# One input tile that holds the last odd pair's strip too, so that a PSUM bank is evacuated in one operation

## The chip, the cores and the metric

The kernel runs on one NeuronCore of a Trainium2 chip. Its engines have instruction queues of their own, worked off in order: TensorE (PE) for matmuls into the PSUM banks, VectorE (DVE), ScalarE (ACT) and GpSimd (POOL) for everything elementwise, SyncE (SP) for issuing DMAs. They wait for one another on semaphores, which a tile framework sets from the tiles that instructions read and write. The metric is the device time of one execution in microseconds, as the median of several runs.

## What is computed

A decaying linear attention, then a first feed-forward layer ("expert") with SiLU, then a second one with a softmax-gated, normalised hidden layer. Inputs: q, k, v, alpha of shape (4, 8, 768, 48), weights (384, 2048), (2048, 384), (384, 1024), (1024, 384) and a gain of 1024. Cut to what matters:

```python
# attention, all float32, for each batch b and head h:
state = 0
for t in range(S):                                   # S = 768, D = 48
    state = alpha[t][:, None] * state + outer(k[t], v[t])
    y[t] = q[t] @ state
x = y as (3072 tokens, 384)
h = x @ w_in;  x = (h * sigmoid(h)) @ w_out          # first expert, 384 -> 2048 -> 384
h = x @ w2_in                                        # second expert, 384 -> 1024 -> 384
e = exp(h - max(h));  solu = h * e / (sum(e) + 1e-9)
ln = (solu - mean(solu)) / sqrt(var(solu) + 1e-6) * g_ln
out = ln @ w2_out
```

## The kernel before

**Attention in chunks.** The 3072 tokens are 24 chunks of 128. For each chunk the class Chunk transposes k (L540), forms scores (L559), masks them, carries the state (L593, L595) and writes the attention's output transposed, heads along the partitions, into two PSUM banks: `y[0]` (bank sA) holds the head pairs 0 and 2, `y[1]` (bank sB) the odd pairs 1 and 3, each as 112 rows by two strips of 128 columns. `evac` (L640, ScalarE) copies a bank to SBUF rounded to the matmul's type, `rest` (L644, VectorE) subtracts that copy from the bank, which leaves the low part: every value is kept as a high and a low half, and each product takes three matmuls.

**Where the output goes.** The first expert reads an input of 384 rows as three blocks of 128 partitions. The 112 rows of a pair leave 16 rows free behind each 48, and the fourth pair is cut up to fill them. `y_all` holds these inputs for two units at a time; a unit is 256 or 384 tokens, eleven in all (UNITS). Bank sA's two strips go straight to blocks 0 and 2 of `y_all`, in one operation of each engine. Of bank sB the first strip goes to block 1, and the second, the last odd pair, to a small tile of its own, `yt`, from which `holes` (L651) copies it by six DMAs into the free rows. So bank sB takes two operations on ScalarE and two on VectorE per chunk (`places`).

**First expert.** For each unit and each of 16 slices of 128 hidden features, `h_groups` makes nine matmuls (L736 to L738), two SiLU activations (L742, L743) and one subtraction for the low half (L746); `x_groups`, two slices later, makes nine matmuls into three accumulators (L771 to L773). After a unit's last slice the accumulators are copied to `x_all` (L779 on VectorE, L781 on ScalarE) and stored to HBM as `x2d[u]` (L783, SyncE). The last unit alone is copied to a tile `x2s` in the pool of the second expert's weights, all three parts by VectorE.

**The order.** The first four units' work is written out by hand in the table ORDER; from there on a chunk's steps are spread evenly between the matmul groups of the unit before. With the last unit the attention's pools are closed and the second expert's weights are loaded (`weight_steps`): eight pieces of 768 KB in a raw form, each loaded by SyncE (L899), converted by ScalarE (L87, L115), VectorE (L93, merge L120), split into high (L932, ScalarE) and low (L937, VectorE). These steps are spread between the matmul groups of the last unit. A raw piece needs a buffer until its merge; two of three lie in the stage pool and every third one uses the space of `x_all` ("spare"), so that piece i + 3 is loaded when piece i is merged.

**Second expert.** 24 tiles of 128 tokens, in an order given by the words HEAD, BODY and TAIL: load and split the input (x; L974, L975), hidden layer (h; 18 matmuls L986 to L988), maximum (m; L146), exponential (e; L149, ScalarE), centring (c; L156 to L162, VectorE), squares (q; L165), factor (f), transposes of the centred tile (t; L1011), high and low copies of them (a, b), output (o; 24 matmuls L1032 to L1034) and store (s). HEAD begins with e0 h1 c0 x2 q0 m1 f0 t0 a0 e1; h0 and m0 are put six matmul groups ahead of the first expert's end. The pool of `y_all`, `x_all` and the SiLU tiles (mw) is closed behind the last group, and the working tiles of the second expert (pool pb: e, s, c, ct and so on) are laid over its space.

Of the kernel before, what the change touches and what calls it, by code (L numbers as in the profile page):

```python
# [4 lines left out]
F32 = mybir.dt.float32  # L5
F32R = mybir.dt.float32r
# [3 lines left out]
U32 = mybir.dt.uint32  # L10
# [9 lines left out]
CH = 128  # L20
HP = 112
# [5 lines left out]
KC, KF, KB = DM // 128, DFF // 128, DF2 // 128  # L27
PW = 768
N1, N2 = 8, 4
W0, W1 = 256, 384  # L30
# [34 lines left out]
NU = len(UNITS)  # L65
# [18 lines left out]
def rebias(nc, f, raw):  # L84


    nc.scalar.mul(f, raw[:, :, 1].bitcast(F32), 2.0**-112)  # L87


def unsign(nc, f, raw=None):  # L90

    if raw is None:
        nc.vector.scalar_tensor_tensor(out=f, in0=f, scalar=-(2.0**32), in1=f, op0=ALU.mult, op1=ALU.max)  # L93
    else:
        spare = raw[:, :, 1].bitcast(F32)
        nc.scalar.activation(out=spare, in_=f, func=AF.Relu, scale=-(2.0**32))
        nc.gpsimd.tensor_tensor(out=f, in0=f, in1=spare, op=ALU.add)
# [15 lines left out]
def low_bits(nc, raw):  # L113

    nc.scalar.mul(raw[:, :, 0], raw[:, :, 0], 2.0**-29 * 0.936)  # L115


def merge(nc, f, raw):
    b = f.bitcast(U32)
    nc.vector.scalar_tensor_tensor(  # L120
        out=b, in0=b, scalar=3, in1=raw[:, :, 0], op0=ALU.logical_shift_left, op1=ALU.bitwise_or
    )
# [7 lines left out]
def words(w):  # L130
    return w.bitcast(U32).rearrange("p (n t) -> p n t", t=2)


class Norm:


    def __init__(self, nc, p, h2, mhalf, tag):
        self.nc, self.p, self.h2, self.mhalf, self.tag = nc, p, h2, mhalf, tag
# [196 lines left out]
def main(tc, const, ident, mask, flags, ones, mhalf, good, x2d,  # L335
# [4 lines left out]
    def push(name):  # L340
        cm = tc.tile_pool(name=name, bufs=1, side="right")
        right.append(cm)
        return cm.__enter__()

    def pop():
        right.pop().__exit__(None, None, None)

    stage, att = push("stage1"), push("att")
# [3 lines left out]
    mw = mw_cm.__enter__()  # L352
# [8 lines left out]
    spare = psh.tile([128, 512], F32, tag="h", name="spare")  # L361
# [8 lines left out]
    v_t, y_t, yt_t, st_t = {}, {}, {}, {}  # L370
# [24 lines left out]
    for t in ms:  # L395
        nc.gpsimd.memset(t, 0.0)

    y_all = mw.tile([128, 2 * KC * 2 * W1], F32R, name="y_all")
    x_all = mw.tile([128, 2 * KC * W0], F32, name="x_all")

    def y_of(u):
        n = UNITS[u][2]
        o = u * KC * 2 * n if u < WIDE else (u - WIDE) % 2 * KC * 2 * n
        return y_all[:, o : o + KC * 2 * n].rearrange("p (k h n) -> p k h n", k=KC, h=2)

    x2s = {}

    def xs_of(u):
        n = UNITS[u][2]
        if u == NU - 1:  # L410
            if "last" not in x2s:
                x2s["last"] = phb.w2.tile([128, KC, n], F32, name="x2s")
            return x2s["last"]
        o = u % 2 * KC * n if u < WIDE else 0
        return x_all[:, o : o + KC * n].rearrange("p (k n) -> p k n", k=KC)

# [103 lines left out]
    class Chunk:  # L520
# [101 lines left out]
        def places(self, k):  # L622

            u, at = self.u, slice(self.at, self.at + CH)
            if u not in y_t:
                y_t[u] = y_of(u)
                yt_t[u] = att.tile([HP, 2, W1], F32R, tag="yt", bufs=1, name="yt")
            y = self.y[k][:HP]
            if k == 0:
                dst = y_t[u][:HP, 0:3:2]  # L630
                return [(y[:, : 2 * CH].rearrange("p (k n) -> p k n", k=2), dst[:, :, 0, at], dst[:, :, 1, at])]
            dst, yt = y_t[u][:HP, 1], yt_t[u]
            return [
                (y[:, CH : 2 * CH], yt[:, 0, at], yt[:, 1, at]),
                (y[:, :CH], dst[:, 0, at], dst[:, 1, at]),
            ]

        def evac(self, k):
            for y, hi, _ in self.places(k):
# [164 lines left out]
    at = {}  # L804
# [8 lines left out]
    phb = None  # L813
    k0 = 0
    for word in ORDER.split():
        letter, i, other = word[0], int(word[1:].rstrip("*")), word[-1] == "*"
# [6 lines left out]
    phb = None  # L823
    for k, (gi, fn) in enumerate(groups):
        if k < k0:
            continue
        fn()
        for s in per.get(k, []):
            s()
        if gi == NG and psh_cm:  # L830
            psh_cm.__exit__(None, None, None)
            psh_cm = None
            phb.open_late(psx)
            nc.scalar.activation(out=act0, in_=act0, func=AF.Exp)
        if phb is None and gi == start[NU - 1] + LAG + 1:
            phb = PhaseB(tc, const, flags, ones, mhalf, good, ident, x2d, w2_in, w2_out, g_ln, out, stage, x_all)
            phb.check(psa)
            psa_cm.__exit__(None, None, None)
            pop()
            pop()  # L840
            phb.stage = push("stage2")
            phb.open_early()
            per.setdefault(len(groups) - 1 - EARLY, []).append(lambda: (phb.h2(0), phb.top(0)))
            ws = phb.weight_steps()
            for i, w in enumerate(ws):
                per.setdefault(k + 1 + (len(groups) - 20 - k) * i // len(ws), []).append(w)
# [7 lines left out]


class PhaseB:
    def __init__(self, tc, const, flags, ones, mhalf, good, ident, x2d, w2_in, w2_out, g_ln, out, stage, spare):
        self.__dict__.update(locals())
        self.nc = tc.nc
        self.cms = []  # L860
# [24 lines left out]
    def weight_steps(self):  # L885
        nc, w2, stage = self.nc, self.w2, self.stage
        self.w2i = w2.tile([128, 2, KC, DF2], F32R, name="w2i")
        self.w2o = w2.tile([128, 2, KB, DM], F32R, name="w2o")
        gl = w2.tile([128, KB], F32, name="gl")
        nc.sync.dma_start(out=gl, in_=self.g_ln)  # L890
        raws = {}

        def load(i):
            if i < 2 * N2:
                if i % 3 == 2:
                    raws[i] = words(self.spare[:, : 2 * PW])
                else:
                    raws[i] = stage.tile([128, PW, 2], U32, tag="raw", bufs=2, name="raw")
                nc.sync.dma_start(out=raws[i], in_=words((self.w2_out if i % 2 else self.w2_in)[i // 2]))  # L899

        fs, parts = {}, {}

        def start(i):
            fs[i] = stage.tile([128, PW], F32, tag="f", bufs=3, name="f")
            rebias(nc, fs[i], raws[i])

        def signed(i):
            low_bits(nc, raws[i])
            unsign(nc, fs[i])

        def joined(i):
            merge(nc, fs[i], raws.pop(i))
            load(i + 3)

        def gained(i):
            if i % 2:
                for j in range(2):
                    k = i // 2 * 2 + j
                    h = fs[i][:, j * DM : j * DM + DM]
                    nc.vector.tensor_scalar_mul(h, h, gl[:, k : k + 1])  # L920

        def split(i):
            f = fs.pop(i)
            if i % 2 == 0:
                k = i // 2 * 256
                hi, lo = (self.w2i[:, q, :, k : k + 256] for q in range(2))
                f = f.rearrange("p (k f) -> p k f", k=KC)
            else:
                k = i // 2 * 2
                hi, lo = (self.w2o[:, q, k : k + 2, :] for q in range(2))  # L930
                f = f.rearrange("p (k f) -> p k f", k=2)
            nc.scalar.copy(hi, f)  # L932
            parts[i] = f, hi, lo

        def lows(i):
            f, hi, lo = parts.pop(i)
            nc.vector.tensor_tensor(out=lo, in0=f, in1=hi.bitcast(F32), op=ALU.subtract)  # L937

        for i in range(3):
            load(i)  # L940
        r = [lambda: None] * 3
        for k in range(2 * N2 + 2):
            for d, fn in ((2, split), (1, signed), (1, joined), (2, lows), (1, gained), (0, start)):
                if 0 <= k - d < 2 * N2:
                    r.append(lambda fn=fn, i=k - d: fn(i))
        return r + [self.first_tiles]
# [184 lines left out]
```

## Time and profile before

| what | us |
|---|---|
| median of three runs (753.98 to 754.39) | 754.22 |
| the profiled execution | 754.29 |
| its span, first to last instruction | 752.5 |
| TensorE busy | 726.6 |
| VectorE busy | 401.7 |
| ScalarE busy | 342.2 |
| GpSimd busy | 147.1 |

The span is what the trace shows; the profiled execution's own time is 1.8 us longer. Busy time counts an engine's instructions while they run, waits not. In a row of a timeline the first two numbers are the start and the duration in microseconds, and what stands in square brackets is the idle time of the engine just before, with whoever ended it. A row "xN" stands for N instructions of a kind that follow each other.

### The profile page before, as it was taken

To read this page: it belongs to the slowest core of one execution; us is meant where nothing else is said; L and a number is where in the kernel's file an instruction comes from. 1 tells how busy PE (TensorE), PEld (TensorE's weight loads), DVE (VectorE), ACT (ScalarE), POOL (GpSimd) and SP (SyncE) were. 2 spreads that over 40 slices of the span, in tenths; PEclk is the share of its full clock that TensorE was granted. 3 is DMA by queue.
4 is the path that set the end of the run, shared out by engine and by line. 5 is a ranking of instruction groups with operands and counts; after the bars stand their busy time and mean duration, and the time that the engine had idled before them with its cause. 6 is when DMAs were issued, how large, how long until landed. Compare 5 with 4: busy or idle time off the path is not lost.

```text
span 752.5 us, 13157 instructions
## 1 busy us (share of the span) xinstructions
PE 726.6 (97%) x5282; PEld 682.2 (91%) x5282; DVE 401.7 (53%) x728; ACT 342.2 (45%) x731; POOL 147.1 (20%) x199
## 2 busy tenths in 40 slices
PE   4779999999999999999999999999999999999996
PEld 3679999999999999999999999999899999999996
DVE  6998963264435335433544422485755555555552
ACT  5768743344344333334333433584544444444442
POOL 4432431222112111111111100001211111111110
PEclk9899999999999999999999999999999999999999
DMA  8645522032122121211402100541211111111001
GB/s 345 206 166 205 183 87 75 13 111 75 54 70 85 54 69 53 86 25 46 138 3 68 43 1 17 203 165 43 74 43 44 42 43 43 43 44 42 32 22 37
DMA packets 27094, 60.11 MB, mean 80 GB/s; under 512 B 3089, under 2 KB 19025, under 8 KB 27025
## 3 DMA queue, kind: packets, MB, share of 16 engines
q1 hardware_dynamic: 26000, 56.28, 21.9%
q10 hardware_dynamic: 1024, 2.92, 1.2%
q8 instruction: 43, 0.70, 0.4%
q14 instruction: 27, 0.21, 0.1%
HBM read 47.39 MB, written 9.44 MB: 76 GB/s over the span
## 4 chain that ended last, share of the span: by engine, by line
PE 92%; DVE 3%; DMA 1%; ACT 1%; issue 1%; POOL 1%; SPq 0%; ACTq 0%; DVEq 0%; POOLq 0%
PE h L736 9%; PE x L771 9%; PE x L773 9%; PE h L738 9%; PE h L737 9%; PE x L772 9%; PE o L1032 5%; PE o L1033 4%; PE h L987 4%; PE h L986 4%; PE o L1034 4%; PE h L988 4%; PE sA L559 3%; PE tp L1011 3%; PE sA L610 1%; PE sA L617 1%
## 5 line engine op out<-in xcount | busy, mean ns | idle before, releaser
L736 PE MATMUL h<-y_all,w1i 128*128 128x384 f32 (+1 forms) x432 | 142.7, 330 | 0.0
L742 ACT ACTIVATE g<-h 128x384 fp32r<-128x384 f32 (+1 forms) x144 | 65.8, 457 | 164.0 <-PE h L738 160.7
L771 PE MATMUL x<-g,w1o 128*128 128x384 f32 (+1 forms) x432 | 138.6, 321 | 0.0
L738 PE MATMUL h<-y_all,w1i 128*128 128x384 f32 (+1 forms) x432 | 138.0, 319 | 0.0
L737 PE MATMUL h<-y_all,w1i 128*128 128x384 f32 (+1 forms) x432 | 137.8, 319 | 0.0
L773 PE MATMUL x<-g,w1o 128*128 128x384 f32 (+1 forms) x432 | 137.3, 318 | 0.1
L772 PE MATMUL x<-g,w1o 128*128 128x384 f32 (+1 forms) x432 | 137.3, 318 | 0.0
L746 DVE TENSOR_TENSOR g<-g,g 128x384 fp32r<-128x384 f32 (+1 forms) x128 | 71.1, 562 | 88.9 <-ACT g L743 86.5
L736 PEld LDWEIGHTS h<-y_all,w1i 128*128 128x128 f32 x432 | 82.4, 191 | 4.2 <-issue 1.7
L771 PEld LDWEIGHTS x<-g,w1o 128*128 128x128 f32 x432 | 81.9, 190 | 2.3 <-issue 2.0
L737 PEld LDWEIGHTS h<-y_all,w1i 128*128 128x128 f32 x432 | 82.6, 191 | 0.0
L738 PEld LDWEIGHTS h<-y_all,w1i 128*128 128x128 f32 x432 | 82.4, 191 | 0.0
L773 PEld LDWEIGHTS x<-g,w1o 128*128 128x128 f32 x432 | 81.8, 189 | 0.3 <-DVE w1o L452 0.3
L772 PEld LDWEIGHTS x<-g,w1o 128*128 128x128 f32 x432 | 81.9, 190 | 0.1
L1032 PE MATMUL o<-w2o,ct 128*128 128x384 f32 x192 | 66.9, 348 | 0.0
L743 ACT ACTIVATE g<-h 128x384 f32<-128x384 f32 (+1 forms) x144 | 65.2, 453 | 1.3 <-POOL g L746 1.3
L1033 PE MATMUL o<-w2o,ct 128*128 128x384 f32 x192 | 64.7, 337 | 0.0
L1034 PE MATMUL o<-w2o,ct 128*128 128x384 f32 x192 | 64.7, 337 | 0.0
L146 DVE TENSOR_REDUCE nm<-h 128x1 f32<-128x1024 f32 x24 | 29.4, 1224 | 58.8 <-PE h L988 58.8
L975 POOL TENSOR_TENSOR x<-x2f,x 128x384 fp32r<-128x384 f32 x24 | 24.4, 1020 | 173.1 <-ACT x L974 173.1
L986 PE MATMUL h<-w2i,x 128*128 128x512 f32 x144 | 57.0, 396 | 0.0
L987 PE MATMUL h<-w2i,x 128*128 128x512 f32 x144 | 56.9, 395 | 0.0
(121 smaller groups left out, 1310.2 us busy)
## 6 DMA issues: line engine op xcount, KB each, us to landing
x<-in_qka_dram SPq DMA_DIRECT2D x20, 768.0 KB, 4.8
raw<-in_w_in_dram SPq DMA_DIRECT2D x11, 768.0 KB, 4.4
raw<-in_w_out_dram SPq DMA_DIRECT2D x11, 768.0 KB, 4.3
v<-in_v_dram SPq DMA_DIRECT2D x24, 200.0 KB, 4.3
x2f<-x2d SPq DMA_DIRECT2D x24, 192.0 KB, 2.8
out_dram<-ob SPq DMA_DIRECT2D x23, 192.0 KB, 1.9
x2d<-x_all SPq DMA_DIRECT2D x5, 576.0 KB, 3.2
x<-in_qka_dram ACTq DMA_DIRECT2D x3, 768.0 KB, 4.2
```

Of the source, the lines that this page charges most:

```text
L736: nc.tensor.matmul(h, w1i[:, 0, kc, fs], Y[:, kc, 0, :n], start=(kc == 0), stop=False)
L737: nc.tensor.matmul(h, w1i[:, 0, kc, fs], Y[:, kc, 1, :n], start=False, stop=False)
L738: nc.tensor.matmul(h, w1i[:, 1, kc, fs], Y[:, kc, 0, :n], start=False, stop=(kc == KC - 1))
L746: eng.tensor_tensor(out=g[:, 1, :n], in0=g32[:, :n], in1=g[:, 0, :n].bitcast(F32), op=ALU.subtract)
L771: nc.tensor.matmul(x, w1o[:, 0, f, msl], g[:, 0, :n], start=first, stop=False)
L772: nc.tensor.matmul(x, w1o[:, 0, f, msl], g[:, 1, :n], start=False, stop=False)
L773: nc.tensor.matmul(x, w1o[:, 1, f, msl], g[:, 0, :n], start=False, stop=last)
L986: nc.tensor.matmul(h[:, sl], x[:, 0, kc, :], self.w2i[:, 0, kc, sl], start=(kc == 0), stop=False)
L987: nc.tensor.matmul(h[:, sl], x[:, 0, kc, :], self.w2i[:, 1, kc, sl], start=False, stop=False)
L1032: nc.tensor.matmul(o, ct[:, 0, kb, :], self.w2o[:, 0, kb, :], start=(kb == 0), stop=False)
L1033: nc.tensor.matmul(o, ct[:, 0, kb, :], self.w2o[:, 1, kb, :], start=False, stop=False)
L1034: nc.tensor.matmul(o, ct[:, 1, kb, :], self.w2o[:, 0, kb, :], start=False, stop=(kb == KB - 1))
```

## The change

The small tile becomes the end of `y_all`, 768 columns further on (`YS`). Both strips of bank sB are then places in one tile, and one access with two steps, the second as far off as the two places are apart, names both: `evac` and `rest` take one operation each for bank sB as for bank sA. The pool mw grows by 3 KB per partition for it. To make room, the last unit's output is no longer copied to a tile `x2s` but to `x_all` as that of the other units, `x_all` no longer serves as the third raw buffer, and piece i + 2 of the second expert's weights is loaded when piece i is merged.

```diff
-    y_all = mw.tile([128, 2 * KC * 2 * W1], F32R, name="y_all")
+    YS = 2 * KC * 2 * W1
+    y_all = mw.tile([128, YS + 2 * W1], F32R, name="y_all")
...
-    x2s = {}
-
     def xs_of(u):
         n = UNITS[u][2]
-        if u == NU - 1:
-            if "last" not in x2s:
-                x2s["last"] = phb.w2.tile([128, KC, n], F32, name="x2s")
-            return x2s["last"]
         o = u % 2 * KC * n if u < WIDE else 0
         return x_all[:, o : o + KC * n].rearrange("p (k n) -> p k n", k=KC)
...
-                yt_t[u] = att.tile([HP, 2, W1], F32R, tag="yt", bufs=1, name="yt")
+                yt_t[u] = y_all[:HP, YS:].rearrange("p (h n) -> p h n", h=2)
...
             dst, yt = y_t[u][:HP, 1], yt_t[u]
-            return [
-                (y[:, CH : 2 * CH], yt[:, 0, at], yt[:, 1, at]),
-                (y[:, :CH], dst[:, 0, at], dst[:, 1, at]),
-            ]
+
+            def both(h):
+
+                a, b = dst[:, h, at], yt[:, h, at]
+                return bass.AP(a.tensor, a.offset, [a.ap[0], [b.offset - a.offset, 2], a.ap[1]])
+
+            return [(y[:, : 2 * CH].rearrange("p (k n) -> p k n", k=2), both(0), both(1))]
...
         def load(i):
             if i < 2 * N2:
-                if i % 3 == 2:
-                    raws[i] = words(self.spare[:, : 2 * PW])
-                else:
-                    raws[i] = stage.tile([128, PW, 2], U32, tag="raw", bufs=2, name="raw")
+                raws[i] = stage.tile([128, PW, 2], U32, tag="raw", bufs=2, name="raw")
...
             merge(nc, fs[i], raws.pop(i))
-            load(i + 3)
+            load(i + 2)
...
-        for i in range(3):
+        for i in range(2):
             load(i)
```

Two places in the programs as built. First ScalarE at the handover from the first expert to the second, with the counters that each instruction waits for (PE, DVE, Pool and Activation stand for the engines, a DMAHW counter for DMAs that have landed). Before:

```order
L743 ACTIVATE g_5466<-h 128x384 [waits DVE_49]
L834 ACT_TABLE_LOAD
L834 ACTIVATE act_101<-act_101 128x1
L149 ACTIVATE e,se<-h_5480,nm 128x1024 [waits DVE_49,PE_49,Activation_49]
L974 CAST x_5567<-x2f 128x384 [waits DMAHW2_49]
L165 ACTIVATE sq,vs<-c 128x1024 [waits DVE_49]
L1016 CAST ct<-tp 128x512 [waits PE_49] x2
L149 ACTIVATE e,se<-h_5537,nm 128x1024 [waits DVE_49]
```

And now, on the same engine:

```order
L741 ACTIVATE g_5411<-h 128x384 [waits DVE_49]
L832 ACT_TABLE_LOAD
L832 ACTIVATE act_101<-act_101 128x1
L149 ACTIVATE e,se<-h_5425,nm 128x1024 [waits DMAHW4_49,DVE_49,Activation_49]
L969 CAST x_5511<-x2f 128x384 [waits DMAHW2_49]
L165 ACTIVATE sq,vs<-c 128x1024 [waits DVE_49]
L1011 CAST ct<-tp 128x512 [waits PE_49] x2
L149 ACTIVATE e,se<-h_5481,nm 128x1024 [waits DVE_49]
```

The order stands; the first exponential (tile e) has lost its wait for TensorE and got one for a DMA counter, whose value there is reached by the store of the last unit from `x_all`. Second the loads of the second expert's weights on SyncE, before:

```order
L899 DMA raw<-in_w_in_dram 128x1536
L899 DMA raw<-in_w_out_dram 128x1536
L899 DMA x_all<-in_w_in_dram 128x1536 [waits DMAHW6_49]
L899 DMA raw<-in_w_out_dram 128x1536 [waits DMAHW0_49,DVE_49]
L899 DMA raw<-in_w_in_dram 128x1536 [waits DMAHW1_49,DVE_49]
```

And now:

```order
L894 DMA raw<-in_w_in_dram 128x1536 [waits DMAHW0_49]
L894 DMA raw<-in_w_out_dram 128x1536 [waits DMAHW1_49]
L894 DMA raw<-in_w_in_dram 128x1536 [waits DMAHW2_49,DMAHW0_49,DVE_49]
L894 DMA raw<-in_w_out_dram 128x1536 [waits DMAHW3_49,DMAHW1_49,DVE_49]
L894 DMA raw<-in_w_in_dram 128x1536 [waits DMAHW4_49,DMAHW2_49,DVE_49]
```

Five of eight loads are shown; the third now waits for VectorE's merge of the first piece, the fourth for that of the second, and so on, each one merge later than before.

## Rows read from the trace of the kernel before

**Rows 1.** The page's first part: busy time, share of the span, instructions.

```profile
PE 726.6 (97%) x5282; PEld 682.2 (91%) x5282; DVE 401.7 (53%) x728; ACT 342.2 (45%) x731; POOL 147.1 (20%) x199
```

**Rows 2.** Busy time by stretches: stretch, its length, busy us of each engine.

```profile
40.00:50.00 10.00, 6.56 (x91) 5.77 (x91) 9.93 (x17) 5.29 (x12) 2.67 (x4) 1.00 0.31 106
...
200.00:300.00 100.00, 100.00 (x778) 95.37 (x778) 43.79 (x76) 38.27 (x91) 18.22 (x20) 1.00 0.19 59
```

**Rows 3.** Timeline of VectorE around one chunk's rest.

```profile
46.72 0.28 DVE L644 TENSOR_TENSOR yt<-sB,yt 112x128 fp32r<-112x128 f32 x1
46.92 0.27 DVE L644 TENSOR_TENSOR y_all<-sB,y_all 112x128 fp32r<-112x128 f32 x1
47.12 0.41 DVE L644 TENSOR_TENSOR y_all<-sA,y_all 112x256 fp32r<-112x256 f32 x1
47.45 0.94 DVE L120 SCALAR_TENSOR_TENSOR f<-f,raw 128x768 uint32<-128x768 uint32 x1
```

**Rows 4.** Chain that ended last, 0 to 60 us: start, us, piece.

```profile
17.11 0.20 DVE yt L644
...
36.41 0.14 ACT yt L640
...
46.72 0.28 DVE yt L644
```

**Rows 5.** Second expert's weights: timelines, landing of the loads, one row of waits.

```profile
500.69 0.33 SPq L899 DMA_DIRECT2D raw<-in_w_out_dram  x1
...
DMA to landing us min/median/max: 4.1/4.3/6.8
...
503.39 0.93 ACT L87 ACTIVATE f<-raw 128x768 f32<-128x768 f32 x1
505.95 0.84 ACT L932 CAST w2o<-f 128x768 fp32r<-128x768 f32 x1 [1.63 <-DVE f L920]
...
513.86 0.55 DVE L746 TENSOR_TENSOR g<-g,g 128x384 fp32r<-128x384 f32 x1
...
514.92 0.33 PE L772 MATMUL x<-g,w1o 128*128 128x384 f32 x1
...
ACT w2o L932 <- DVE f L920: 6.6, 4, 2.6
```

**Rows 6.** Handover: timelines, landing of stores (last unit's; all, L783), chain's transposes.

```profile
527.01 1.12 ACT L149 ACTIVATE e<-h,nm 128x1024 f32<-128x1024 f32 x1 [6.56 <-DVE x2s L779]
...
527.55 0.34 SPq L783 DMA_DIRECT2D x2d<-x2s  x1
...
x2d<-x2s SPq DMA_DIRECT2D x1, 576.0 KB, 2.8
...
DMA to landing us min/median/max: 2.3/3.1/4.7
...
529.71 0.75 DVE L160 TENSOR_SCALAR c<-s,mu 128x1024 f32<-128x1024 f32 x1
...
535.32 0.76 DVE L160 TENSOR_SCALAR c<-s,mu 128x1024 f32<-128x1024 f32 x1
...
531.13 0.87 PE tp L1011 x8
...
536.22 1.06 PE tp L1011 x8
```

**Rows 7.** An earlier gap of TensorE; then stretches of 1 us: PE busy, granted clock.

```profile
49.14 0.34 PE L559 MATMUL sA<-x 48*128 48x128 f32 x1 [2.87 <-DVE x L483]
...
49.00:50.00 1.00, 0.86 (x15) 1.00 0.43 84
50.00:51.00 1.00, 1.00 (x11) 0.67 0.29 57
51.00:52.00 1.00, 1.00 (x6) 0.50 0.86 186
...
53.00:54.00 1.00, 1.00 (x7) 0.62 0.67 268
```

More of the change, by code (lines that the diff above doesn't have):

```diff
@@ L835, in main @@
         if phb is None and gi == start[NU - 1] + LAG + 1:
-            phb = PhaseB(tc, const, flags, ones, mhalf, good, ident, x2d, w2_in, w2_out, g_ln, out, stage, x_all)
+            phb = PhaseB(tc, const, flags, ones, mhalf, good, ident, x2d, w2_in, w2_out, g_ln, out, stage)
             phb.check(psa)
@@ L856, with __init__ @@
 class PhaseB:
-    def __init__(self, tc, const, flags, ones, mhalf, good, ident, x2d, w2_in, w2_out, g_ln, out, stage, spare):
+    def __init__(self, tc, const, flags, ones, mhalf, good, ident, x2d, w2_in, w2_out, g_ln, out, stage):
         self.__dict__.update(locals())
```

## The prediction

> **What bounds the kernel now.** I read the page first. TensorE is busy for 97% of the span [rows 1], and the chain of work that ended last runs through its matmuls nearly everywhere. The busy table by stretches shows where the other 3% lies: TensorE is full in stretches such as 200 to 300 us, but works for only 6.56 of the 10 us from 40 to 50, where VectorE works for 9.93 [rows 2]. From 50 us on TensorE has no gap to speak of until the last tiles, so a time saved on VectorE or ScalarE in there is worth nothing unless TensorE waits for it. So three places have to be priced: the first 50 us, where the changed evacuations can lie on the path; the loading of the second expert's weights (480 to 519 us), where a buffer goes; and the handover to the second expert (527 to 536 us), where the tile x_all gets a new user.
>
> **Evacuation in one operation.** For each of 24 chunks ScalarE and VectorE now issue one operation over 2 x 128 columns in place of two over 128. Such an operation is in the trace: bank sA is evacuated that way. On VectorE, start to start, the two small ones take 46.72 to 47.12, 0.40 us, and the double one 47.12 to 47.45, 0.33 us [rows 3]. That saves 0.07 us a chunk. Fifteen chunks lie where TensorE is full: nothing. Of the nine at the start the chain holds a pair of bank sB at four places between 17.11 and 46.72 us (three of them are in [rows 4]; the one at 36.41 is on ScalarE, priced alike). That is 4 x 0.07 = 0.28 us; some of it is caught again by waits for GpSimd and for weights behind it, so I take -0.2. Bounds: +0.1, since a pair's first half is now ready only with its second, and -1.3, if all nine chunks count on both engines (18 x 0.07).
>
> [...]
>
> **The small tile and the holes.** The copies from the small tile into the rows left free wait for the same operations and run on the same queues as before. The new access touches only its two strips, and the program as built has no new wait between it and the matmuls that read the other unit. I cost this at nothing.
>
> **Two raw buffers in place of three.** A load of the second expert's weights is now issued one piece later. The latest is the load of piece 6, issued when piece 4 is merged, at 500.69. Alone it lands about 4.3 us later, at 505.0, while its conversion on ScalarE stood at 503.39 [rows 5]. So ScalarE waits up to 1.6 us, with the activations of the first expert queued behind the waiting instruction, VectorE behind them, and TensorE behind both. Two things cover it. ScalarE stood idle for 1.63 us before the next split (505.95), and TensorE takes the low half that VectorE finished at 513.86 + 0.55 = 514.41 only at 514.92: 0.5 us of cover [rows 5]. If nothing of the 1.6 us fell into that idle time, 1.6 - 0.5 = 1.1 us would reach TensorE; if all did, nothing. Pieces 2 and 4 slip too, by less. Near the lower end, I take +0.2, bounds 0 and 1.1.
>
> **The last unit's output in x_all.** This is the term that decides. Before, the last unit was copied to a tile of its own (x2s). Now it goes to x_all, which lies in a pool whose space the second expert's working tiles take over. The program as built shows what that costs: the first exponential on ScalarE no longer waits for the last matmul of the first expert, but for the store of x_all to HBM. In the trace that exponential starts at 527.01; the store is issued at 527.55 and lands 2.8 us later, at 530.35 [rows 6]. So it starts at about 530.4, 3.4 us late.
>
> Queued behind it on ScalarE are the split of the next input, the squares, the copies of the transposed tile and the next exponential; VectorE's centring waits for it, and TensorE's transposes for that. Centring ends at 529.71 + 0.75 = 530.46, and becomes 533.86. TensorE reached the first transposes at 531.13 without waiting [rows 6]; with the 0.14 us from the end of a centring to the transpose (second tile: 535.32 + 0.76 = 536.08, transpose at 536.22 [rows 6]) they now start at 534.0, and TensorE idles for 2.87 us. It makes nothing of this good: the second transposes stood directly behind the second centring, and that one hangs on squares, copies and the second exponential, all behind the first exponential in ScalarE's queue. They come about 3.3 us late, at 539.5, while the matmuls in between end at 534.0 + 0.87 + 4.2 = 539.1 (4.2 is what lay between the two groups of transposes, 532.0 to 536.2). After that TensorE is full again and the tile period is set by it. **+3.3 us**, bounds 2.6 and 3.8 (the stores from x_all landed in 2.3 to 4.7 us with a median of 3.1 [rows 6]; the ends allow the 2.8 us to be 0.7 shorter or 0.5 longer).
>
> [...]
>
> **The clock.** TensorE idled for 2.87 us once before, ahead of 49.14. It resumed at the full clock, but the granted clock fell to 0.50 (1.2 GHz) at about 50.3 (a mean of 0.67 in 50 to 51) and was back at 1.00 near 53.8 (0.62 in 53 to 54): some 3.4 us at half rate, 1.7 us lost [rows 7]. The new gap has that same length and follows a stretch of full work. So I expect a fall here too. Of its 1.7 us, 0.4 us is hidden while the second transposes wait for the second centring (539.1 to 539.5): **+1.2 us**, bounds 0 and 1.7.
>
> **The sum.** The profiled execution took 754.29 us (its span is 752.5), and the median of the three runs is 754.22, so nothing has to be corrected. 754.3 - 0.2 + 0.2 + 3.3 + 1.2 = 758.8 us.
>
> **Rivals.** *Rival A: the handover without the fall of the clock.* The clock need not fall after every gap of that length. Then 754.3 - 0.2 + 0.2 + 3.3 = 757.6. For it: one example is little evidence. Against it: the length agrees to the hundredth.
>
> *Rival B: the weights come late.* If the conversions' waits add up down ScalarE's queue and the 0.5 us of cover goes too, TensorE stalls for the whole 1.6 us in 480 to 519 us: 758.8 - 0.2 + 1.6 = 760.2, or above. Against it: ScalarE stood idle for 6.6 us in all ahead of four splits in there [rows 5].
>
> *Rival C, not slower: the store is through in time.* The wait costs nothing if the store lands before TensorE runs out of work. The second transposes have no slack, so the loss is 0.54 us (527.55 - 527.01) plus the landing time, less 0.1. To stay within 1.5 us of before, the store would have to land in 1.1 us or less. Then 754.3 - 0.2 + 0.2 + 1.0 = 755.3, and with the upper bound of the evacuations 754.2. Against it: the fastest of nine such stores took 2.3 us.
>
> **How the numbers follow.** Forecast (wait and fall of the clock) 0.60, rival A 0.27, rival B 0.07, rival C 0.06. The forecast's own bounds are 756.8 (754.3 - 1.3 + 0 + 2.6 + 1.2) and 761.0 (754.3 + 0.1 + 1.1 + 3.8 + 1.7), if every bound falls to one side, which is unlikely. Rival A is wanted inside for the most part. I take 756.7 to 760.2. A measurement of this kernel can tell some 0.2% (1.5 us) from no change. Forecast and rivals A and B lie above 755.7; of rival C I give 0.04 to no change and 0.02 to faster. Slower: 0.94.
>
> **What would show it.** In the profile after: the idle time before the first exponential grows by 3.4 us to about 10 us, and its releaser is the store of x_all; the first transposes start near 534.0 behind a gap of about 2.9 us, and the granted clock falls behind it. If TensorE shows no gap there, the handover term is wrong. If the gap is there with the clock at 1.00, it is rival A. If the x_all store has landed and the exponential still starts at 527.0, the wait was no wait. In the first 50 us the transposes of chunk 4 at 50.3 should come 0.2 us earlier, and between 480 and 519 us ScalarE's waits for loads appear before the conversions of pieces 2, 4 and 6, with TensorE's gaps under half a microsecond in sum.

## The result, and the profile after

| | before | after |
|---|---|---|
| median of four runs each, us | 754.10 (752.54 to 754.39) | 758.57 (758.51 to 758.95) |
| ratio, 95% interval | | 1.006 (1.0047 to 1.0072) |
| the profiled execution, us | 754.29 | 758.95 |
| its span, us | 752.5 | 757.2 |

The change makes the kernel slower by 4.5 us, 0.6%. The forecast was 758.8. Its largest term, the wait of the first exponential for a store, stands in the trace as it was priced. Its second, the fall of the clock behind that wait, stands there too, but the experiments show that it comes in some executions of the same kernel and not in others, so that its place in a median is partly chance, and so is an agreement to 0.2 us.

The page's first part, after, answers to [rows 1]: VectorE has 24 instructions less, ScalarE too, and the busy times of both hardly change.

```profile
PE 730.2 (96%) x5282; PEld 684.8 (90%) x5282; DVE 401.6 (53%) x704; ACT 341.4 (45%) x707; POOL 147.7 (20%) x199
```

TensorE is busy for 3.6 us more with the same 5282 matmuls. That is a first hint of the clock.

**The handover.** The rows that answer to [rows 6], from the timelines of VectorE, SyncE, ScalarE and TensorE (in brackets the idle time before, and who ended it):

```profile
526.75 1.60 DVE L777 COPY x_all<-x 128x384 f32<-128x384 f32 x3 [0.86 <-PE x L771]
528.38 0.34 SPq L781 DMA_DIRECT2D x2d<-x_all  x1
531.27 1.12 ACT L149 ACTIVATE e<-h,nm 128x1024 f32<-128x1024 f32 x1 [9.98 <-DMA x2d<-x_all]
533.96 0.75 DVE L160 TENSOR_SCALAR c<-s,mu 128x1024 f32<-128x1024 f32 x1
534.82 1.06 PE L1006 MATMUL tp<-ident,c 128*128 128x128 f32 x8 [2.85 <-issue]
539.45 0.75 DVE L160 TENSOR_SCALAR c<-s,mu 128x1024 f32<-128x1024 f32 x1
541.46 1.04 PE L1006 MATMUL tp<-ident,c 128*128 128x128 f32 x8
```

Read them from the top. The last unit's three copies to x_all end at 528.35, and the store is issued at once. ScalarE's first exponential had 6.56 us of idle time before it, ended by a copy; now it has 9.98 us, ended by the store. It starts 2.89 us after the store's issue. Centring follows 2.7 us behind it and TensorE's first transposes 0.1 us behind that. TensorE, which did not wait there at all, stands idle for 2.85 us.

The busy table by stretches of 1 us shows the clock there (columns: PE, PE's weight loads, VectorE, ScalarE, GpSimd, then the granted clock, the DMA share and GB/s):

```profile
534.00:535.00 1.00, 0.18 (x2) 0.21 (x3) 0.96 (x4) 0.25 (x1) 0.00 (x0) 1.00 0.00 0
535.00:536.00 1.00, 1.00 (x9) 0.98 (x8) 1.00 (x1) 1.00 (x3) 0.00 (x0) 0.90 0.59 176
536.00:537.00 1.00, 1.00 (x4) 0.74 (x3) 0.97 (x4) 1.00 (x3) 0.40 (x1) 0.50 0.07 21
537.00:538.00 1.00, 1.00 (x4) 0.81 (x3) 0.69 (x3) 1.00 (x3) 0.37 (x2) 0.50 0.00 0
538.00:539.00 1.00, 1.00 (x3) 0.78 (x3) 1.00 (x1) 0.37 (x1) 0.56 (x1) 0.50 0.00 0
539.00:540.00 1.00, 1.00 (x5) 0.82 (x4) 0.93 (x4) 0.00 (x0) 0.45 (x1) 0.89 0.00 0
```

TensorE resumes at 534.82 at the full clock (1.00 in 534 to 535), and about 1 us later the granted clock is 0.50 until about 539.2. The hidden layer's matmuls start 0.43 us apart there; in run 8 below, the same kernel with the clock at 1.00, it is 0.23. For the kernel before the clock is 1.00 throughout this stretch.

**Where the 4.7 us of span went.** I cut the span at four instructions that every variant has: the merge on VectorE that follows the last evacuation of the start phase (L120, near 47 us), the range check behind the last attention chunk (L870 before, L868 after; near 476 us), the first copy of the last unit's output (near 526 us), and the second tile's transposes (tp, 536.22 before [rows 6]). In the trace of the change these are VectorE's rows

```profile
46.08 0.41 DVE L642 TENSOR_TENSOR y_all<-sB,y_all 112x256 fp32r<-112x256 f32 x1
46.42 0.41 DVE L642 TENSOR_TENSOR y_all<-sA,y_all 112x256 fp32r<-112x256 f32 x1
46.75 0.94 DVE L120 SCALAR_TENSOR_TENSOR f<-f,raw 128x768 uint32<-128x768 uint32 x1
...
476.50 0.17 DVE L868 TENSOR_SCALAR ok<-flags 112x24 f32<-112x24 f32 x1
```

and the rows at 526.75 and 541.46 above.

| stretch, us | before | after | difference |
|---|---|---|---|
| start to the merge | 47.45 | 46.75 | -0.70 |
| merge to the range check (attention, first expert) | 428.57 | 429.75 | +1.18 |
| range check to the last unit's copies (weights) | 49.90 | 50.25 | +0.35 |
| copies to the second transposes (handover) | 10.30 | 14.71 | +4.41 |
| from there to the end | 216.28 | 215.74 | -0.54 |
| span | 752.5 | 757.2 | +4.7 |

The handover alone gives 4.41 of 4.7 us. The experiments tell what of the other lines is the change and what is scatter.

### The profile page after: what moved, and what is told of

The parts are those of the page before. It is cut to its first block, busy times and chain, and to the rows that moved or that the text cites. A ratio compares the mean times of both kernels' runs of the same rounds, so it can differ in the third digit from the quotient of the medians.

```text
span 757.2 us, 13092 instructions
## 1 busy us (share of the span) xinstructions
PE 730.2 (96%) x5282; PEld 684.8 (90%) x5282; DVE 401.6 (53%) x704; ACT 341.4 (45%) x707; POOL 147.7 (20%) x199
```

## The experiments

Each variant was compared with the kernel before on the same chip. The theory under test is that the wait for the store at the handover is the loss, because x_all lies in the pool whose space the second expert's working tiles take over; the rivals are the loss of the third raw buffer, and the clock.

**1. The change with x_all in a pool of its own.** The new pool is closed only behind the second expert, so that expert's working tiles get other space.

```diff
+    mx_cm = tc.tile_pool(name="mx", bufs=1)
+    mx = mx_cm.__enter__()
     mw_cm = tc.tile_pool(name="mw", bufs=1)
...
-    x_all = mw.tile(
+    x_all = mx.tile(
...
     phb.close()
+    mx_cm.__exit__(None, None, None)
```

> The change, with x_all in a pool of its own that is closed behind the second expert, so that no working tile lies over it. The last unit is still stored from x_all, two raw buffers stay, the evacuation stays in one operation. Theory W (the first exponential's wait for the store, 3.3 us, and the fall of the clock behind it, 1.2 us, make the loss): the exponential starts right behind the last matmul of the first expert, TensorE shows no gap near 531, and the time is 4.4 us under the changed kernel's 758.6, near 754.2. Theory L (the two raw buffers make it): stays near 758.6. Theory V (the merged evacuation or the new layout of the input tile makes it): stays near 758.6.

Measured: 753.9 us (751.96 to 755.94) against 754.02 (752.85 to 755.87) before, ratio 1.000 (0.9988 to 1.0013). The loss is gone. ScalarE's timeline shows why; the last unit still goes to x_all, but the exponential's idle time ends with the copy:

```profile
525.36 1.12 ACT L149 ACTIVATE e<-h,nm 128x1024 f32<-128x1024 f32 x1 [6.55 <-DVE x_all L779]
```

That is the row of before, 6.56 us and a copy [rows 6]. The store is made all the same; it only has nobody waiting for it.

**2. The kernel before with only the last unit's output moved to x_all.** Three raw buffers, two evacuations, no x2s.

```diff
-        if u == NU - 1:
-            if "last" not in x2s:
-                x2s["last"] = phb.w2.tile([128, KC, n], F32, name="x2s")
-            return x2s["last"]
```

> The kernel before with one part of the change: the last unit's output goes to x_all in the pool mw in place of x2s. Three raw buffers (x_all still serves as the third) and the separate evacuations stay. Theory W: the whole loss comes back, 754.1 + 4.4 = 758.5 us, with a gap of TensorE of 2.9 us near 531 and the granted clock at 0.50 for some 3.4 us behind it. Theories L and V: 754.1, since neither the buffers nor the evacuation is touched.

Measured: 757.87 us (756.81 to 759.33), ratio 1.005 (1.0031 to 1.0068). That is 3.85 us over the kernel before, where the whole change had 4.47 in its first comparison and 3.25 in the second (run 8): these four lines carry the loss. The chain of work that ended last shows the new path, 525.95 to 539.56 us (start, us, piece), with no matmul in it until the transposes:

```profile
525.95 1.61 DVE x_all L773 x3
...
527.58 2.79 DMA x2d<-x_all
...
530.47 1.22 ACT e L149 x2
...
531.71 1.24 DVE s L156 x2
...
533.16 0.76 DVE c L160
...
533.95 1.16 ACT sq L165 x2
...
536.06 1.12 ACT e L149 x2
...
538.66 0.76 DVE c L160
...
539.56 1.06 PE tp L1005 x8
```

This is the queue that the prediction named: store, exponential, centring, squares, copies, second exponential, second centring, second transposes. From the copies to those transposes it takes 13.61 us against 10.30, so +3.31. And the clock stayed at 1.00 here, behind a gap of TensorE of 2.86 us: rival A, in this execution.

**3. The kernel before with only two raw buffers.**

```diff
-                if i % 3 == 2:
-                    raws[i] = words(self.spare[:, : 2 * PW])
-                else:
-                    raws[i] = stage.tile([128, PW, 2], U32, tag="raw", bufs=2, name="raw")
+                raws[i] = stage.tile([128, PW, 2], U32, tag="raw", bufs=2, name="raw")
...
-            load(i + 3)
+            load(i + 2)
```

> The kernel before with one part of the change: two raw buffers for the second expert's weights in place of three. Theory W: +0.2 to +0.4 us, near 754.4, with ScalarE waiting 1.4 to 1.6 us for the loads of pieces 2, 4 and 6. Theory L: +4 us, near 758. Theory V: 754.1.

Measured: 754.36 us (753.26 to 756.63), ratio 0.9998 (0.9986 to 1.0011): nothing that the medians can tell. In its trace the weights stage takes 50.45 us against 49.90.

**4. The change with x_all in its own pool and as third raw buffer again.** Loads and waits are then those of before, and the evacuation in one operation is what is left of the change. Beside the new pool of experiment 1:

```diff
-                raws[i] = stage.tile([128, PW, 2], U32, tag="raw", bufs=2, name="raw")
+                if i % 3 == 2:
+                    raws[i] = words(self.spare[:, : 2 * PW])
+                else:
+                    raws[i] = stage.tile([128, PW, 2], U32, tag="raw", bufs=2, name="raw")
...
-            load(i + 2)
+            load(i + 3)
```

> The change with x_all in a pool of its own and with x_all as the third raw buffer again: of the change the evacuation in one operation is left, and the last unit's way through x_all without its wait. Theory W: 754.1 - 0.2 = 753.9 us, as fast as before or a shade faster, and 0.2 to 0.4 us faster than the kernel with two raw buffers and the same pool. Theory L: 754.1. Theory V: near 758.6.

Measured: 753.47 us (751.63 to 755.53), ratio 0.9993 (0.9982 to 1.0005). What the evacuation saves can't be told from nothing in the time; the traces tell it, below.

**5. The change with the last store in three parts**, each behind its own copy. This makes the wait shorter and leaves all else.

```diff
-                    if m == KC - 1 and f == KF - 1:
+                    if u == NU - 1:
+                        nc.sync.dma_start(out=x2d[u][:, m], in_=xs[:, m])
+                    elif m == KC - 1 and f == KF - 1:
                         nc.sync.dma_start(out=x2d[u], in_=xs)
```

> The change, but the last unit is stored from x_all in three parts, each behind its own copy. The theory says that the first exponential starts when the last part has landed. Stores of 192 KB (out) land in 1.9 us in the trace of the change, that of 576 KB in 2.85, so the exponential should start 0.9 us earlier against the last copy, TensorE's gap ahead of the first transposes should be 1.9 us instead of 2.85, and the time 0.9 us less than the change's if the clock behaves alike, about 757.6. If a gap of 1.9 us does not bring the clock down behind it, another 1 us or so is saved: 756.6. The rival, that the first exponential is late for another reason (the space of x_all has to be free of VectorE's copies), expects no difference.

Chain, exponential and transposes in its trace:

```profile
527.66 1.88 DMA x2d<-x_all
...
529.65 1.12 ACT L149 ACTIVATE e<-h,nm 128x1024 f32<-128x1024 f32 x1 [9.08 <-DMA x2d<-x_all]
...
533.20 1.06 PE L1008 MATMUL tp<-ident,c 128*128 128x128 f32 x8 [1.96 <-issue]
538.74 1.06 PE L1008 MATMUL tp<-ident,c 128*128 128x128 f32 x8 [0.27 <-DVE se L161]
```

The last third lands in 1.88 us in place of 2.79, the gap is 1.96 us in place of 2.86, and the handover takes 12.71 us in place of 13.61: 0.9 us each time, as expected. The clock did not fall. The median, 757.26 us (755.17 to 758.48), lies 0.3 us under the unaltered change's on the same chip (757.58); single runs of either scatter by over 3 us, so the medians say nothing on 0.9 us, and the trace decides.

**6. The change with its gap filled** by ten matmuls whose result nobody uses.

```diff
-        steps(HEAD)
+        head = HEAD.split()
+        steps(" ".join(head[:2]))
+        warm = self.psx.tile([128, 512], F32, tag="x2", name="warm")
+        for _ in range(10):
+            nc.tensor.matmul(warm, self.w2i[:, 0, 0, :128], self.w2i[:, 0, 0, :512], start=True, stop=True)
+        steps(" ".join(head[2:]))
```

> The change, with ten more matmuls of 512 columns (results unused) on TensorE between the hidden layer of tile 1 and the first transposes of the second expert. They take some 2.3 us of the gap of 2.85 us, and nothing that is waited for is behind them. The theory's forecast (a wait of 3.3 us, and 1.1 us by the clock that falls behind the gap) expects no fall of the clock in 534 to 541 us and about 757.4. If the fall costs nothing or is no consequence of the gap, the time stays at the change's 758.5, and the clock in 535 to 539 us reads as before or falls all the same.

TensorE's timeline:

```profile
530.67 2.46 PE L1057 MATMUL warm<-w2i 128*128 128x512 f32 x10
533.69 1.06 PE L1006 MATMUL tp<-ident,c 128*128 128x128 f32 x8 [0.56 <-issue]
539.23 1.06 PE L1006 MATMUL tp<-ident,c 128*128 128x128 f32 x8 [0.27 <-DVE se L161]
```

The gap shrinks to 0.56 us, the clock stays at 1.00, and the handover still takes 13.61 us: keeping TensorE at work does not bring the exponential forward. 756.99 us (756.18 to 759.18), ratio 1.0039 (1.0025 to 1.0054), against 757.58 for the unaltered change. The expectation was built on the change having a fall; as experiment 8 shows, it need not have one, so this run by itself doesn't show that the filling prevents it.

**7. The change with the last store made twice**, the second behind the landing of the first: the wait doubled.

```diff
-                        nc.sync.dma_start(out=x2d[u], in_=xs)
+                        for _ in range(2 if u == NU - 1 else 1):
+                            nc.sync.dma_start(out=x2d[u], in_=xs)
```

> The change, with the last unit's store issued twice, the second one behind the landing of the first; the first exponential then waits for both. If the landing of the store sets the end, it starts one landing later, 2.9 us, TensorE's gap is 5.7 us and the time 2.9 us above the change's: about 761.4. If TensorE can make some of a wait good, or if another wait holds the exponential, it is less: with another wait by more than 1 us less.

Chain, exponential and first transposes in its trace:

```profile
527.12 2.79 DMA x2d<-x_all
...
529.93 2.77 DMA x2d<-x_all
...
532.80 1.11 ACT L149 ACTIVATE e<-h,nm 128x1024 f32<-128x1024 f32 x1 [12.77 <-DMA x2d<-x_all]
...
536.35 1.94 PE L1007 MATMUL tp<-ident,c 128*128 128x128 f32 x8 [5.64 <-DVE se L161]
```

761.1 us (760.91 to 763.21), ratio 1.010 (1.0084 to 1.0117), 3.5 us above the unaltered change on the same chip; 2.9 were expected. The handover takes 17.38 us. Of the 3.76 us over 13.62, the second landing is 2.8, and the rest is the clock, which fell here, this time before TensorE resumed: the eight transposes take 1.94 us in place of 1.06. The first transposes are the better place to compare, since the clock has cost nothing up to there. They start 7.17 us behind the first of the three copies in experiment 5, 8.08 in run 8 and 10.85 here, where the store took 1.88, 2.79 and 2.79 + 2.77 us. So in these traces every microsecond that the store takes longer is a microsecond of wait.

**8. The change again**, beside 5 to 7, and three further profiled executions (9 to 11); a further one of the filled gap (12).

> The change unaltered, beside the three others on one chip. By the medians so far 758.5. In the run with only the store from x_all the clock stayed at 1.00 behind a gap of 2.86 us and the second transposes came 3.34 us late; in the change's own trace it fell to 0.50 for 3.3 us and they came 4.4 us late. If the fall comes in some executions and not in others, the single times lie in two groups about 1.1 us apart, on top of what the kernel before scatters.

> The change unaltered, one look, to see whether TensorE's clock falls behind the gap at the handover in this execution. From the last copies of the first expert to the second transposes of the second the kernel before took 10.30 us; without a fall 13.6 us are expected (10.3 + 3.3), with a fall 14.6.

> As e9_change_look: 13.6 us without a fall of the clock, 14.6 with one. If the fall were fixed by the gap's length, it would come in all of these looks or in none.

> As e9_change_look: 13.6 us without a fall of the clock, 14.6 with one.

> The filled gap of e6_filled_gap, one more look: no fall of the clock behind it, and 13.6 us from the last copies to the second transposes.

Run 8: 757.58 us (755.62 to 760.11) against 754.33 (752.97 to 755.77), ratio 1.0046 (1.0032 to 1.0061). That is 3.25 us, 1.2 less than in the first comparison (the intervals overlap). The single times are spread evenly, not in two groups as expected, so the medians don't show that the fall makes up these 1.2 us. The traces show that the handover differs from execution to execution. Transposes and stretches of 1 us of run 8 (the same kernel as the one of the section above):

```profile
533.93 1.06 PE L1006 MATMUL tp<-ident,c 128*128 128x128 f32 x8 [2.87 <-issue]
539.47 1.06 PE L1006 MATMUL tp<-ident,c 128*128 128x128 f32 x8 [0.27 <-DVE se L161]
...
535.00:536.00 1.00, 1.00 (x5) 0.77 (x5) 0.97 (x4) 1.00 (x4) 0.29 (x1) 1.00 0.24 70
536.00:537.00 1.00, 1.00 (x6) 0.81 (x5) 0.81 (x2) 1.00 (x3) 0.48 (x2) 1.00 0.00 0
```

and of run 11:

```profile
534.17 1.41 PE L1006 MATMUL tp<-ident,c 128*128 128x128 f32 x8 [2.87 <-issue]
540.84 1.03 PE L1006 MATMUL tp<-ident,c 128*128 128x128 f32 x8
...
535.00:536.00 1.00, 1.00 (x5) 0.91 (x4) 0.97 (x4) 1.00 (x4) 0.05 (x1) 0.50 0.53 157
536.00:537.00 1.00, 1.00 (x4) 0.80 (x3) 1.00 (x2) 1.00 (x2) 0.71 (x2) 0.50 0.00 0
```

The gap is 2.87 us in both. In run 8 the clock stays full and TensorE waits another 0.27 us for the second centring; in run 11 it falls, TensorE comes late to the second transposes and finds them ready. The handover takes 13.62 us in the one, 14.75 in the other. Run 9 took 759.88 us and is like run 11 at the handover (14.73), run 10 took 756.64 and is like run 8 (13.62); run 11 took 758.27. Run 12, filled, took 757.75 and shows no fall and 13.61. The kernel before took 753.34 beside these four. That the fall came in some executions and not in others with the gap unchanged rules out that its length alone fixes it.

**All traces, cut at the same four instructions** (us; the fall columns say where the granted clock was 0.50 near 50 us and at the handover):

| trace | to merge | to range check | fall near 50 | weights | handover | fall there | rest | span |
|---|---|---|---|---|---|---|---|---|
| before | 47.45 | 428.57 | 50 to 54 | 49.90 | 10.30 | no | 216.28 | 752.5 |
| the change | 46.75 | 429.75 | 48 to 55 | 50.25 | 14.71 | yes | 215.74 | 757.2 |
| 1 own pool | 46.05 | 428.06 | no | 50.15 | 10.31 | no | 215.63 | 750.2 |
| 2 only store | 47.34 | 428.56 | 51 to 55 | 50.05 | 13.61 | no | 215.94 | 755.5 |
| 3 two raws | 47.77 | 429.87 | 49 to 56 | 50.45 | 10.30 | no | 216.21 | 754.6 |
| 4 merged, three raws | 46.04 | 428.06 | no | 49.95 | 10.30 | no | 215.55 | 749.9 |
| 5 three stores | 47.18 | 428.55 | 50 to 54 | 50.30 | 12.71 | no | 215.76 | 754.5 |
| 6 filled gap | 47.35 | 428.05 | no | 50.22 | 13.61 | no | 215.57 | 754.8 |
| 7 store twice | 47.24 | 428.08 | no | 50.18 | 17.38 | yes | 216.22 | 759.1 |
| 8 the change | 47.49 | 428.06 | no | 50.30 | 13.62 | no | 216.43 | 755.9 |
| 9 the change | 46.74 | 429.85 | 48 to 55 | 50.53 | 14.73 | yes | 216.25 | 758.1 |
| 10 the change | 46.95 | 428.06 | no | 50.34 | 13.62 | no | 215.93 | 754.9 |
| 11 the change | 47.38 | 428.57 | 50 to 54 | 50.14 | 14.75 | yes | 215.66 | 756.5 |
| 12 filled gap | 47.60 | 428.55 | 50 to 54 | 50.38 | 13.61 | no | 215.76 | 755.9 |

Read the handover column alone: 10.30 wherever x_all is not waited for, 13.61 where it is, 0.9 less with the shorter store, 2.8 more with the longer one, and 1.1 more where the clock falls. No other column sorts the kernels that way.

## Why the prediction was right, point by point

- **The wait for the store, +3.3 us (bounds 2.6 and 3.8): 3.3 measured.** 13.61 or 13.62 less 10.30, in the five traces that wait for one store of 576 KB and kept the clock (2, 6, 8, 10, 12). The steps hold too: exponential 2.89 us behind the store's issue, centring, transposes 0.1 us behind it, a gap of 2.85 (2.87 forecast), nothing made good up to the second transposes. The row of 2.8 us was the right price: the store took 2.79 us in the chains of experiments 2 and 7. The kernel has nine units, not eleven, so the nine stores of the prediction are all there are. Experiments 1 and 2 show that the place of x_all is the cause: with its own pool the loss goes, with the store alone it comes.
- **The fall of the clock, +1.2 us (bounds 0 and 1.7): 1.1 where it comes.** In the five profiled executions of the change it came three times (14.71, 14.73, 14.75) and stayed out twice (13.62, 13.62). The size came out nearly right, in a sum that has two errors. 1.7 less 0.4 is 1.3, not 1.2. And the 1.7 us took matmuls to run at half rate. In the fall near 50 us in the trace of before, at 0.50, matmuls of 256 columns start 0.214 us apart (51.20 to 53.34), and behind it, at 1.00, 0.12 us apart (54.01 to 57.97): a factor of 1.8. No view gives a frequency; the one that the prediction puts beside the 0.50 agrees with an estimate from that spacing, 256 columns in 0.214 us, 1.2 a nanosecond. At the handover, in the change's trace, nine steps from start to start of the hidden-layer matmuls behind the transposes take 3.72 us (535.64 to 539.36), in run 8 2.19 (534.75 to 536.94), so the fall cost 1.53. The 0.4 us that the second centring hides holds: in run 8 the second transposes start 0.67 us behind the last hidden-layer matmul's start (538.80), 0.44 more than the spacing of 0.23; 1.53 less 0.44 is the 1.1 that was measured. What was wrong is the reason that the equal length of the gap gave: 2.85 to 2.87 us of idle time in all five, and 2.86 in run 2, decide nothing. Nor did the fall near 50 us, which was the example, cost 1.7: the traces with such a fall are 0.5 us longer there than those without. Forecast and rival A are two outcomes of one kernel. So the median of a few runs can come out near either: 758.57 in the first four, 757.58 in the nine of run 8, where rival A had 757.6. All thirteen have a mean of 758.1, between the forecast and rival A.
- **The weights with two raw buffers, +0.2 us (bounds 0 and 1.1): +0.3.** The weights column is 49.90 to 50.05 in the three traces with three raw buffers (before, 2, 4) and 50.14 to 50.53 in the eleven with two, some 50.3 in the mean. ScalarE's timeline of the change shows the wait before pieces 2, 4 and 6, as forecast. Piece 6 was to wait for up to 1.6 us and the others for less; they wait about equally:

```profile
489.69 0.92 ACT L87 ACTIVATE f<-raw 128x768 f32<-128x768 f32 x1 [1.47 <-DMA raw<-in_w_in_dram]
497.56 0.91 ACT L87 ACTIVATE f<-raw 128x768 f32<-128x768 f32 x1 [1.57 <-DMA raw<-in_w_in_dram]
506.04 0.91 ACT L87 ACTIVATE f<-raw 128x768 f32<-128x768 f32 x1 [1.42 <-DMA raw<-in_w_in_dram]
...
ACT f L87 <- DMA raw<-in_w_in_dram: 5.1, 4, 1.6
ACT w2o L927 <- DVE f L915: 2.6, 1, 2.6
```

  The last two rows, of the table of waits in 480 to 520 us (total, times, longest), show the cover at work: the waits for loads came to 5.1 us (0.6 of it before piece 0, as in the kernel before), and ScalarE's waits before the splits went from 6.6 us [rows 5] to 2.6. Rival B, a stall of 1.6 us, did not come.
- **The evacuations, -0.2 us (bounds +0.1 and -1.3): about -0.17.** The rows of VectorE at 46 us above are bank sB in one operation and bank sA, 0.34 and 0.33 us start to start, as [rows 3] had it for sA. From TensorE's first matmul behind its wait for GpSimd (27.84 before) to the merge it takes 19.61 us before and in run 2, 19.90 in run 3, which evacuate in two operations; in nine of eleven traces that evacuate in one it takes 19.43 to 19.46, in two 19.65 and 19.72. The longest of each kind, runs 3 and 9, show the same waits of TensorE on the way (0.3 us for VectorE, 0.9 for GpSimd) and differ by 0.18 us, like the rest. Of the change's -0.70 us in that stretch, 0.55 had come before that matmul, which is scatter. The gain of 0.17 us is 0.02% of the time, and nothing shows of it in the medians.
- **The rest is scatter that fell out even.** The change's trace gained 0.55 us before the first such matmul and 0.54 us behind the second transposes, and lost 1.18 us where the clock fell near 50 us earlier and for longer than in the trace of before. The runs of the change without that fall (8, 10) are not late there. None of it is the change's, and the prediction rightly had nothing for it; but that the sum met the median to 0.2 us owes something to this, and to how often the fall came, which the prediction could not know.

What stays open: when the clock falls and when not. Filled gaps showed no fall in two executions, but open gaps showed none in three of six either (2, 8 and 10 against the change, 9 and 11), so that filling helps is likely and not shown. The last stretch varies from 215.6 to 216.4 us, but not in TensorE's work: from the second transposes to the end of the last matmul all fourteen traces take 209.56 to 209.65 us, and the 5.93 to 6.86 us behind it, with the last copy and its store, hold the whole difference. Why they vary no experiment tells. The traces of experiments 1 and 4 reach the merge first of all (46.05 and 46.04 us); they are those of the fastest of their twelve executions, so this says nothing for the pool.

## What to carry to other kernels

Look where a tile lies, not only who reads and writes it: when its pool's space passes to the next stage, the next stage's first write inherits a wait for the tile's last reader, and where that is a store to HBM it is a wait for the landing (2.8 us here for 576 KB), at the one point where every engine is waiting for the first result. A pool of its own for the one tile that is stored last took the loss away and kept all the rest of the change. And cut traces at a few fixed instructions before comparing spans: here the span of one kernel scatters by 3.2 us (754.9 to 758.1 in five traces of the change), while the stretch that matters repeats to 0.04 us with the clock alike.

## What the hardware showed that was not expected

**The clock falls at varying places in one and the same program.** In all five traces of the change TensorE is idle for 2.8 us near 47 and for 2.85 to 2.87 us at the handover. Yet the granted clock fell near 48 us and at the handover in two of them (the first and 9), near 50 and at the handover in one (11), and at neither in two (8 and 10). What a fall costs is not set by its length alone. From the merge to the range check the traces take 428.05 to 428.08 us without a fall near 50, 428.55 to 428.57 with one that begins at 50 or 51, and 429.75 to 429.87 with one from 48 or 49 to 55: 0.5 or 1.7 us for about 3.4 or 6.8 us at 0.50. At the handover a fall of about 3.4 us (535.8 to 539.2 in the change's first trace) cost 1.1 (14.71 less 13.62).

**Early in the span the granted clock reads 1.00 where matmuls run at the low rate.** Run 8's matmuls of 256 columns, and one stretch of 1 us of it:

```profile
31.67 0.41 PE L736 MATMUL h<-y_all,w1i 128*128 128x256 f32 x1
31.88 0.41 PE L734 MATMUL h<-y_all,w1i 128*128 128x256 f32 x1
...
37.21 0.28 PE L736 MATMUL h<-y_all,w1i 128*128 128x256 f32 x1
37.33 0.28 PE L734 MATMUL h<-y_all,w1i 128*128 128x256 f32 x1
...
31.00:32.00 1.00, 0.89 (x4) 0.92 (x5) 1.00 (x2) 0.59 (x2) 0.77 (x1) 1.00 0.93 190
```

They start 0.21 us apart near 31 and 0.12 apart near 37, with the clock at 1.00 in the row of 31. The kernel before has the same 0.21 near 31, and there its row reads 0.50; and near 51, where a fall stands in its rows, it has 0.21 as well. So these matmuls ran at the low rate in both, and only one of the profiles says so. The first matmuls of all, near 8 us, where the clock reads 1.00 in every trace, are spaced like those near 28 us (0.21 us between those into one bank, before and after). From 49 to 57 us and at the handover the rows and the spacings agree in all fourteen traces, so the falls counted above stand. Where the slow spacing ends is not the same in each trace: run 9 leaves it at 30.7 us, amid its first group of such matmuls, run 8 only behind that group (32.95).

**A store's landing depends on its size only in part.** 576 KB landed in 2.79 us, 192 KB in 1.88 (the 23 stores of `out` of that size that SyncE issues have a median of 1.9), so a third of the bytes took two thirds of the time. An estimate from these two rows, if they differ by their bytes alone: 393,216 bytes more in 0.91 us are 432 GB/s; at that rate 192 KB would take 0.45 us, which leaves 1.4 us of the 1.88 that does not go with the size.
